# The modulation product of an adaLN block, contracted in chunks of 128, 128, 128 and 64 rows instead of four of 112

## The chip, the cores and the metric

The kernel runs on one core of a Trainium2 chip. The metric is the device time of one execution in microseconds (us). The core has five engines with a queue each, which work their instructions off in order: PE (TensorE, the matrix array; its weight loads are shown apart as PEld), DVE (VectorE), ACT (ScalarE), POOL (GpSimd) and SP (SyncE, which here only issues DMA transfers). ACT's queue issues a few DMAs as well. The queues are shown in the profile as SPq and ACTq where a DMA is issued. SBUF is the on-chip memory with 128 partitions, PSUM the accumulators that PE writes.

## The reference, cut to what matters

```python
def ref(A_x, A_wqkv, A_wo, B_w1, B_b1, B_w2, B_b2, c, w_mod):   # S = 2048, D = 448, F = 1792, H = 16
    mod = (silu(c) @ w_mod).reshape(1, 6, 1, 448)               # c: (1, 448), w_mod: (448, 6 * 448)
    sa, ca, ga, sb, cb, gb = (mod[:, i] for i in range(6))
    h = layernorm(x) * (1 + ca) + sa
    x = x + ga * attention(h, A_wqkv, A_wo)                     # 16 heads of 28, full softmax
    h = layernorm(x) * (1 + cb) + sb
    x = x + gb * (gelu(layernorm(h) @ B_w1 + B_b1) @ B_w2 + B_b2)
    return x
```

All values are float32. The change touches only `silu(c) @ w_mod`: a product of one row of 448 with a matrix of 448 x 2688.

## The kernel before, in words

The order of instructions on every engine is written out by hand in the program; no scheduler reorders it. Tokens are worked in four blocks of 512 (`acc[0]` to `acc[3]`). The first 175 us (phase 1) project q, k and v and take score maxima, the next 580 us or so are attention, the rest is the output projection and the MLP.

**The modulation product before.** The 448 rows of the contraction lie on partitions, in `NC = 4` chunks of `CK = 112`. `c` is loaded as a tile of 112 x 4 (line 132, the first DMA of SP's queue), ACT applies Silu (L138), and DVE copies the result 32 times side by side, so that each chunk is a 112 x 32 weight tile `sil_b` (L293). PE then makes, for each output row of 448 numbers, one matmul per chunk. An output j goes to PSUM partitions 32j to 32j + 31, that is to its own group of 32 columns of the array.

- *First part, `sa` and `ca`* (the shift and scale of the first layernorm): four loads of 112 x 896 at line 154 into `wm_ac`, which lies in the slots c0 and c1 (the profile's `slot_c`). After 24 matmuls that only keep PE busy (L297, they need nothing but the identity), eight matmuls stand at L300, each of them two records in the profile. ACT copies the result out of PSUM (L306), DVE copies 64 of its columns (L307), PE transposes it (L313), and ACT writes the columns `sa_col` and `ca_col` (L316, L317).
- *Second part, `ga, sb, cb, gb`*: `mod_load(k)` at line 562 loads 112 x 1792 into slots v2 and v3, and `mod_mm(k)` makes four matmuls per chunk (L569), one for each of the tasks 0 to 3 of block 1 in phase 1. `mod_fin` brings the result to DRAM and back as rows (L576 to L582).

**The start of the kernel.** SP issues, in this order: `c`, the first half of `acc[0]`, the four loads of `wm_ac`, the q and k weights (L148 to L150), `acc[1]`, the v weights, `acc[2]` and `acc[3]`. ACT's queue issues the second half of `acc[0]`. Eight semaphores go round among the DMAs, so the ninth issue waits until the first transfer has landed, the tenth for the second, and so on. DVE's first work of weight is the copy L293; the layernorm statistics of block 0 (`ln1`, L184 and L185) stand behind it on DVE, then the reciprocal root on POOL (L191), and the normalised tiles come alternately from DVE (L201, L209) and from ACT (L217, L218). On ACT, Silu needs an ACT_TABLE_LOAD ahead of it. ACT's queue then holds: L217, L218, L217, L218, L306, the first weight cast L178, L316, L317, and the copies L282 that apply `sa` and `ca` to the transposed tiles.

On PE the order is L297, L300, eight transposes (L261), L313, eight more transposes, and the q projection (L618, L631, L338). L618 needs the tiles that DVE rounds from L282's output (L285).

The weights of q, k and v are already loaded in the other form: three chunks of 128 rows, and the last 64 rows to both halves of the partitions (L148 to L150).

Of the kernel before, what the change touches and what calls it, by code (L numbers as in the profile page):

```python
# [13 lines left out]
F32 = mybir.dt.float32  # L14
# [8 lines left out]
D = 448  # L23
H = 16
DH = 28
F = 1792
CK = 112
NC = D // CK
NB = S // 512
NG = H // 4  # L30
NKT = S // 128
# [10 lines left out]
def tile_adaln_block(ctx: ExitStack, tc: tile.TileContext, x, wqkv, wo, w1, b1, w2, b2, c, w_mod, out):  # L42
    nc = tc.nc
    pe, act, dve, pool, sp = nc.tensor, nc.scalar, nc.vector, nc.gpsimd, nc.sync
# [27 lines left out]
    def nm(t):  # L72
        uid[0] += 1
        return f"{t}_{uid[0]}"

    def sbt(tag, shape, dt=F32, bufs=1):
        return sb.tile(shape, dt, tag=tag, name=nm(tag), bufs=bufs)

    def slot(tag, shape, dt=F32R):
        return sb.tile(shape, dt, tag="slot_" + tag, name=nm("slot_" + tag), bufs=1)  # L80
# [4 lines left out]
    def slot4(tag, inner):  # L85
        if tag not in halved:
            t = slot(tag, [128, 4] + inner)
            return lambda k: t[:, k]
        t2 = [slot(tag + h, [128, 2] + inner) for h in ("", "h")]
        return lambda k: t2[k // 2][:, k % 2]  # L90
# [6 lines left out]
    def ps_s():  # L97
        return ps_tile("pa", 2)
# [5 lines left out]
    def ps_o():  # L104
        return ps_tile("o")
# [4 lines left out]
    def f(t):  # L110
        return t.bitcast(F32)
# [16 lines left out]


    cols = sbt("cols", [128, 4 * NC])  # L130
    c_col, sil, sa_col, ca_col = cols[:CK, 0:NC], cols[:CK, NC : 2 * NC], cols[:, 2 * NC : 3 * NC], cols[:, 3 * NC :]
    sp.dma_start(c_col, c[0].rearrange("(k p) -> p k", p=CK))
    acc = [sbt(f"acc{b}", [128, 4, D]) for b in range(NB)]

    xv = x[0].rearrange("(b p t) n -> b p t n", p=128, t=4)
    for h in range(2):
        (act if h else sp).dma_start(acc[0][:, 2 * h : 2 * h + 2, :], xv[0][:, 2 * h : 2 * h + 2, :])
    act.activation(sil, c_col, AF.Silu)  # L138

    raw_qk = [slot(f"v{1 + i}", [128, 2, 2 * D], F32) for i in range(2)]  # L140
    raw_v = slot("v3", [128, NC, D], F32)

# [3 lines left out]
    def load_w(cs, dst):  # L146
        for k in range(3):
            sp.dma_start(dst(k), wqkv[128 * k : 128 * k + 128, cs])  # L148
        sp.dma_start(dst(3)[0:64], wqkv[384:D, cs])
        sp.dma_start(dst(3)[64:128], wqkv[384:D, cs])  # L150

    wm_ac = [slot(f"c{i}", [CK, 2, 2 * D], F32) for i in range(2)]
    for k in range(NC):
        sp.dma_start(wm_ac[k // 2][:, k % 2, :], w_mod[k * CK : (k + 1) * CK, 0 : 2 * D])
    load_w(slice(0, 2 * D), lambda k: raw_qk[k // 2][:, k % 2, :])
    sp.dma_start(acc[1], xv[1])
    load_w(slice(2 * D, 3 * D), lambda k: raw_v[:, k, :])
# [5 lines left out]
    wq = [[slot4(f"a{2 * kind + part}", [H, 32]) for part in range(2)] for kind in range(2)]  # L163
    wv = [slot(f"e{part}", [128, NC, D]) for part in range(2)]
    for kind in range(2):
        for part in range(2):
            for k in range(NC):
                pool.memset(f(wq[kind][part](k))[:, :, DH:32], 0.0)
# [120 lines left out]


    d0 = slot("d0", [128, 4, 512], F32)
    sil_b = d0[:CK, 0, 0 : NC * 32].rearrange("p (k r) -> p k r", r=32)
    dve.tensor_copy(sil_b, sil[:, :, None].broadcast_to([CK, NC, 32]))  # L293
    pm = ps_s()
    warm = ps_s()
    for _ in range(WARM):
        pe.matmul(warm[:, :128], ident, ident, start=True, stop=True)  # L297
    for k in range(NC):
        for j in range(2):
            pe.matmul(  # L300
                pm[32 * j : 32 * j + 32, :D], sil_b[:, k, :], wm_ac[k // 2][:, k % 2, j * D : (j + 1) * D],
                start=(k == 0), stop=(k == NC - 1),
            )
    xs0 = ln1(0)
# [253 lines left out]
    mod = {}  # L558

    def mod_load(k):  # L560
        mod[k] = slot(f"v{2 + k % 2}", [128, 4 * D], F32)
        sp.dma_start(mod[k][:CK], w_mod[k * CK : (k + 1) * CK, 2 * D :])

    def mod_mm(k):
        if k == 0:
            mod["p"] = ps_o()
        p = mod["p"]
        for j in range(4):
            pe.matmul(  # L569
                p[32 * j : 32 * j + 32, :D], sil_b[:, k, :], mod[k][:CK, j * D : (j + 1) * D],  # L570
                start=(k == 0), stop=(k == NC - 1),
            )

# [48 lines left out]
    for n, i in (  # L622
# [7 lines left out]
        p, ts = firsts[n]  # L630
# [3 lines left out]
    for b in range(NB):  # L634
# [13 lines left out]
        for n, (tb, kind, g) in enumerate(tasks):  # L648
# [9 lines left out]
            k = n - (6, 5, 4, 4)[b]  # L658
# [16 lines left out]
            if more:  # L675
                k = n - (6, 5, 4, 4)[b]
# [11 lines left out]
            if n == 6:  # L688
                v_init(b)
                if b == 0:  # L690
                    mod_load(0)
                    mod_load(1)
            if b == 2 and n == 5:
                sp.dma_start(b1_col, b1.rearrange("(k p) -> p k", p=128))
            if b == 1:
                if n < 2:
                    mod_mm(n)
                    mod_load(2 + n)
                elif n in (2, 3):
                    mod_mm(n)  # L700
                    if n == 3:
                        mod_fin()
# [348 lines left out]
    def n_maxima(s_):  # L1051
        n_plain, n_wo = left_steps(s_)
        over = len(mxq) - 7 * n_plain // 2
        if is_wo(s_):
            return max(0, -(-over // max(n_wo, 1)))
        plain[0] += 1
        return 4 if plain[0] % 2 or (over > 3 * n_wo and over > 0) else 3
# [11 lines left out]
    for u in range(NU):  # L1069
        g, qt = divmod(u, NB)  # L1070
        for kt in range(NKT):
# [10 lines left out]
            n = n_maxima(step)  # L1082
# [81 lines left out]
    for n in range(len(seq) + LAG):  # L1164
        if n < len(seq):
            b, i = seq[n]
# [38 lines left out]
```

## Time and profile before

| | |
|---|---|
| median of 3 runs | 1142.74 us (1142.39 to 1142.86) |
| profiled execution | 1142.82 us, of which its span 1141.0 us |
| outside the span | 1.8 us |
| PE busy | 1132.1 us, 99% of the span |
| DVE, ACT, POOL busy | 830.5, 680.9, 216.5 us |
| moved by DMA | 81.08 MB, mean 71 GB/s |
| granted PE clock | full in all 40 slices |

The profile shows one execution. Times in it count from the start of the span. In a timeline each line gives start, duration, engine, source line, operation, `out<-in`, the number of instructions merged, and in brackets how long the engine had been idle and what ended that wait. In a view of stretches, each line gives the stretch, the busy time of the engines, the clock, the busy share of the 16 DMA engines and the rate in GB/s. "The chain" is the sequence of work that ended last, traced back from the last instruction.

### The profile page before, as it was taken

How to read it: one execution, taken by the hardware profiler on the slowest of the kernel's cores; microseconds unless marked ns; L12 is line 12 of the kernel's file. 1: busy time of each engine (PE TensorE's matmuls, PEld its weight loads, DVE VectorE, ACT ScalarE, POOL GpSimd, SP SyncE). 2: the span in 40 equal slices, each digit the busy share in tenths (PEclk: the TensorE clock that was granted, in tenths of full speed). 3: DMA queues.
4: the chain of work that ended last, by engine and by line, in shares of the span. 5: the costliest groups of instructions: out<-in, count | busy, mean ns of one | idle time of the engine just before them, and what ended most of it. 6: DMA issues, size and time to landing. Idle time of an engine off the chain costs nothing.

```text
span 1141.0 us, 20798 instructions
## 1 busy us (share of the span) xinstructions
PE 1132.1 (99%) x8380; PEld 682.0 (60%) x8380; DVE 830.5 (73%) x1487; ACT 680.9 (60%) x836; POOL 216.5 (19%) x235
## 2 busy tenths in 40 slices
PE   9999999999999999999999999999999999999998
PEld 7767774444444444444444445545458888888887
DVE  6958788999989899989899977595448853444322
ACT  5666767777877787878787877576862321211110
POOL 2533341110000000000000010207114503123000
PEclk9999999999999999999999999999999999999999
DMA  8652254121231211221111212020423100000000
GB/s 301 205 181 93 94 185 117 51 67 38 67 102 52 62 40 45 78 69 60 52 48 57 91 61 75 11 84 1 135 55 87 43 34 1 1 33 1 33 1 33
DMA packets 49345, 81.08 MB, mean 71 GB/s; under 512 B 12616, under 2 KB 18588, under 8 KB 49248
## 3 DMA queue, kind: packets, MB, share of 16 engines
q1 hardware_dynamic: 48768, 79.01, 22.0%
q8 instruction: 66, 1.08, 0.4%
q10 hardware_dynamic: 144, 0.46, 0.1%
q0 software_dynamic: 336, 0.28, 0.1%
q14 instruction: 31, 0.25, 0.1%
HBM read 53.11 MB, written 26.35 MB: 70 GB/s over the span
## 4 chain that ended last, share of the span: by engine, by line
PE 96%; DVE 1%; DMA 1%; ACT 0%; issue 0%; POOL 0%; DVEq 0%; POOLq 0%; SPq 0%
PE s L1092 27%; PE o L1062 22%; PE m L338 16%; PE pa L338 10%; PE m L415 6%; PE s L1155 4%; PE s L1156 4%; PE s L1154 4%; PE ma L415 1%; PE o L261 1%; PE pa L297 1%; DVE mxp L420 1%; PE m L261 1%; DMA drec<-den 0%; DMA osb<-drec 0%
## 5 line engine op out<-in xcount | busy, mean ns | idle before, releaser
L420 DVE TENSOR_REDUCE mxp<-m 128x1 f32<-128x512 f32 x882 | 556.2, 684 | 105.0 <-PE m L415 79.3
L1092 PE MATMUL s<-slot_b,slot_a 32*128 32x512 f32 x3072 | 384.6, 423 | 0.1
L1097 ACT ACTIVATE slot_c<-s 128x1024 f32<-128x1024 f32 x340 | 329.5, 1022 | 83.7 <-PE s L1092 83.0
L1092 PEld LDWEIGHTS s<-slot_b,slot_a 32*128 32x128 f32 x3072 | 216.2, 183 | 250.9 <-ACT slot_c L1097 148.5
L415 PE MATMUL m<-kh,qh 32*128 32x512 f32 x852 | 282.5, 472 | 0.7 <-DVE mxp L420 0.5
L1097 ACT ACTIVATE slot_d<-s 128x1024 f32<-128x1024 f32 x172 | 166.7, 1021 | 42.0 <-PE s L1092 41.9
L1062 PE MATMUL o<-slot_c,v 128*32 128x512 f32 x1360 | 181.2, 605 | 0.0
L1138 ACT ACTIVATE full<-m,b_col 128x512 f32<-128x512 f32 x56 | 38.5, 688 | 192.1 <-PE m L338 179.8
L1141 DVE CAST hi<-full 128x512 fp32r<-128x512 f32 x56 | 25.2, 450 | 135.4 <-ACT full L1138 135.4
L415 PEld LDWEIGHTS m<-kh,qh 32*128 32x128 f32 x852 | 111.7, 182 | 7.5 <-DVE mxp L420 4.2
L828 POOL TENSOR_TENSOR osb<-osb,osb 128x512 f32<-128x512 f32 x16 | 20.9, 1307 | 445.0 <-DMA osb<-drec 303.0
L1062 PE MATMUL o<-slot_d,v 128*32 128x512 f32 x688 | 92.5, 605 | 0.4 <-ACT osb L1031 0.4
L338 PE MATMUL m<-y,slot_a 128*128 128x512 f32 x160 | 60.6, 395 | 0.0
L1062 PEld LDWEIGHTS o<-slot_c,v 128*32 128x32 f32 x1360 | 26.8, 108 | 54.2 <-issue 52.7
L1142 DVE TENSOR_TENSOR lo<-full,hi 128x512 fp32r<-128x512 f32 x56 | 44.1, 788 | 5.2
L338 PE MATMUL m<-y,slot_c 128*128 128x512 f32 x152 | 47.5, 396 | 0.1
L428 ACT ACTIVATE slot_d<-m 128x512 f32<-128x512 f32 x43 | 24.4, 597 | 37.4 <-PE ma L415 19.7
L1156 PE MATMUL s<-slot_v,lo 128*128 128x448 f32 x128 | 46.7, 365 | 0.0
L1154 PE MATMUL s<-slot_v,hi 128*128 128x448 f32 x128 | 46.6, 364 | 0.0
L338 PE MATMUL m<-y,slot_v 128*128 128x512 f32 x112 | 39.2, 396 | 0.0
L338 PE MATMUL m<-y,slot_b 128*128 128x512 f32 x112 | 39.0, 398 | 0.0
L338 PE MATMUL pa<-slot_c,slot_a 128*128 128x512 f32 x136 | 36.8, 404 | 0.0
(252 smaller groups left out, 1449.6 us busy)
## 6 DMA issues: line engine op xcount, KB each, us to landing
d<-lo SPq DMA_DIRECT2D x32, 256.0 KB
slot_b<-d SPq DMA_DIRECT2D x32, 256.0 KB
slot_a<-d SPq DMA_DIRECT2D x32, 256.0 KB
d<-hi SPq DMA_DIRECT2D x20, 256.0 KB
osb<-drec SPq DMA_DIRECT2D x15, 256.0 KB
out_dram<-xn SPq DMA_DIRECT2D x16, 224.0 KB
slot_v<-in_w_mod_dram SPq DMA_DIRECT2D x4, 784.0 KB
raw<-in_B_w_dram SPq DMA_DIRECT2D x14, 224.0 KB
```

The source lines that it names most:

```text
L338: pe.matmul(p, a, b, start=(i == 0), stop=(i == len(terms) - 1))
L415: pe.matmul(m, qh_sb[(g, qt)][js, i * 128 : (i + 1) * 128], k[js, :], start=True, stop=True)
L420: dve.tensor_reduce(out=mxp[(g, qt)][:, i, j, cch : cch + 1], in_=m, op=ALU.max, axis=AX.X)
L1062: pe.matmul(o[32 * j : 32 * j + 32, :], v_sb[kt // 4][:, kt % 4, 4 * g + j, :], p[:, j, :], start=(kt == 0), stop=(kt == NKT - 1),)
L1092: pe.matmul(s2[:, jj, :], ks[rows_, kp, kc], qs[rows_, qp, :], start=(term == 0), stop=(term == 2))
L1097: act.activation(pt[:, 2 * hf : 2 * hf + 2, :], s2, AF.Exp, scale=SCALE)
L1138: act.activation(gf, p, AF.Gelu_apprx_tanh, bias=b1_col[:, i : i + 1])
L1141: dve.tensor_copy(ghi, gf)
L1142: dve.tensor_tensor(out=glo, in0=gf, in1=f(ghi), op=ALU.subtract)
L1154: pe.matmul(pp, ghi[:, ts], w_hi, start=(m == 0), stop=False)
L1155: pe.matmul(pp, ghi[:, ts], w_lo, start=False, stop=False)
L1156: pe.matmul(pp, glo[:, ts], w_hi, start=False, stop=(m == NFT - 1))
```

## The change

The contraction is cut into chunks of 128, 128, 128 and 64 rows. The last chunk is split by output: the first half of the outputs takes its 64 rows of `w_mod` on partitions 0 to 63, the second half on partitions 64 to 127, and the last 64 numbers of `c` are loaded to both halves. So the last chunk is two loads of 64 rows, each half as wide. The number of matmuls and their widths stay. The loads of `c` move behind the halves of `acc[0]`: 128 x 3 numbers on SP's queue, and two loads of 64 numbers on ACT's queue, ahead of Silu.

```diff
-CK = 112
-NC = D // CK
+NC = 4
...
-    c_col, sil, ... = cols[:CK, 0:NC], cols[:CK, NC : 2 * NC], ...
-    sp.dma_start(c_col, c[0].rearrange("(k p) -> p k", p=CK))
+    c_col, sil, ... = cols[:, 0:NC], cols[:, NC : 2 * NC], ...
...
     for h in range(2):
         (act if h else sp).dma_start(acc[0][:, 2 * h : 2 * h + 2, :], xv[0][:, 2 * h : 2 * h + 2, :])
+
+    sp.dma_start(c_col[:, 0:3], c[0, 0:384].rearrange("(k p) -> p k", p=128))
+    for h in range(2):
+        act.dma_start(c_col[64 * h : 64 * h + 64, 3:4], c[0, 384:D].rearrange("(p k) -> p k", k=1))
     act.activation(sil, c_col, AF.Silu)
...
-    wm_ac = [slot(f"c{i}", [CK, 2, 2 * D], F32) for i in range(2)]
+    def load_mod(dst, k, c0, n):
+        if k < 3:
+            sp.dma_start(dst[:, : n * D], w_mod[128 * k : 128 * k + 128, c0 : c0 + n * D])
+        else:
+            for h in range(2):
+                x0 = c0 + h * n * D // 2
+                sp.dma_start(dst[64 * h : 64 * h + 64, : n * D // 2], w_mod[384:D, x0 : x0 + n * D // 2])
+
+    def mod_part(k, j, n):
+        if k < 3:
+            return slice(0, 128), slice(j * D, (j + 1) * D)
+        h, j = divmod(j, n // 2)
+        return slice(64 * h, 64 * h + 64), slice(j * D, (j + 1) * D)
+
+    wm_ac = [slot(f"c{i}", [128, 2, 2 * D], F32) for i in range(2)]
     for k in range(NC):
-        sp.dma_start(wm_ac[k // 2][:, k % 2, :], w_mod[k * CK : (k + 1) * CK, 0 : 2 * D])
+        load_mod(wm_ac[k // 2][:, k % 2, :], k, 0, 2)
...
-    sil_b = d0[:CK, 0, 0 : NC * 32].rearrange("p (k r) -> p k r", r=32)
-    dve.tensor_copy(sil_b, sil[:, :, None].broadcast_to([CK, NC, 32]))
+    sil_b = d0[:, 0, 0 : NC * 32].rearrange("p (k r) -> p k r", r=32)
+    dve.tensor_copy(sil_b, sil[:, :, None].broadcast_to([128, NC, 32]))
...
         for j in range(2):
+            rs_, cs = mod_part(k, j, 2)
             pe.matmul(
-                pm[32 * j : 32 * j + 32, :D], sil_b[:, k, :], wm_ac[k // 2][:, k % 2, j * D : (j + 1) * D],
+                pm[32 * j : 32 * j + 32, :D], sil_b[rs_, k, :], wm_ac[k // 2][rs_, k % 2, cs],
                 start=(k == 0), stop=(k == NC - 1),
...
-        sp.dma_start(mod[k][:CK], w_mod[k * CK : (k + 1) * CK, 2 * D :])
+        load_mod(mod[k], k, 2 * D, 4)
...
         for j in range(4):
+            rs_, cs = mod_part(k, j, 4)
             pe.matmul(
-                p[32 * j : 32 * j + 32, :D], sil_b[:, k, :], mod[k][:CK, j * D : (j + 1) * D],
+                p[32 * j : 32 * j + 32, :D], sil_b[rs_, k, :], mod[k][rs_, cs],
```

In the changed program the two waits for the small loads of `c` on ACT's queue stand ahead of the ACT_TABLE_LOAD; the wait for the load on SP's queue stands behind it, at Silu itself. On SP's queue the two half loads of the last chunk of `wm_ac` wait for the two halves of `acc[0]`, the q and k weights' first three loads for the three loads of `c`. Elsewhere the order of instructions on every engine is as it was.

More of the change, by code (lines that the diff above doesn't have):

```diff
@@ L130, in tile_adaln_block @@
     cols = sbt("cols", [128, 4 * NC])
-    c_col, sil, sa_col, ca_col = cols[:CK, 0:NC], cols[:CK, NC : 2 * NC], cols[:, 2 * NC : 3 * NC], cols[:, 3 * NC :]
-    sp.dma_start(c_col, c[0].rearrange("(k p) -> p k", p=CK))
+    c_col, sil, sa_col, ca_col = cols[:, 0:NC], cols[:, NC : 2 * NC], cols[:, 2 * NC : 3 * NC], cols[:, 3 * NC :]
     acc = [sbt(f"acc{b}", [128, 4, D]) for b in range(NB)]
```

## The prediction

> **What bounds the kernel now.** I read the page first, then the chain in order of time for the first 31 us, then the timeline of the same stretch, then the DMA rates there, and last the places of the second part. From the page: the span, the busy shares, the clock by slices and the chain by engine.
>
> ```profile
> span 1141.0 us, 20798 instructions
> PE 1132.1 (99%) x8380; PEld 682.0 (60%) x8380; DVE 830.5 (73%) x1487; ACT 680.9 (60%) x836; POOL 216.5 (19%) x235
> PEclk9999999999999999999999999999999999999999
> PE 96%; DVE 1%; DMA 1%; ACT 0%; issue 0%; POOL 0%; DVEq 0%; POOLq 0%; SPq 0%
> ```
>
> PE is the chain almost everywhere, at the full granted clock. So a microsecond added to PE's path at the start, or put between two PE instructions, is a microsecond at the end, and a load that becomes faster behind PE is worth nothing. The change touches two places: the first 16 us, and four short matmul groups between 61 and 75 us. The chain through the first place (start, length, what):
>
> ```profile
> 1.36 8.17 PE pa L297 x48
> 9.53 3.13 PE pa L300 x16
> 12.66 1.02 PE ma L261 x8
> 13.69 0.40 PE pa L313 x4
> 14.11 0.16 ACT cols L316
> 14.38 0.79 ACT raw L282
> 15.19 0.44 DVE slot_b L285
> 15.77 3.40 PE pa L618 x12
> ```
>
> The fillers L297 run to 9.53, then the modulation matmuls, eight transposes, the transposes of the modulation, ACT, DVE, and the first projection. The loads are not in it. The same stretch on the other engines (timeline; in brackets the idle time before and its releaser):
>
> ```profile
> 0.74 0.41 ACTq L137 DMA_DIRECT2D acc<-in_A_x_dram  x1
> 1.19 1.28 ACT L138 ACT_TABLE_LOAD   x1 [1.19 <-PEq L1192]
> 4.57 0.20 ACT L138 ACTIVATE cols<-cols 112x4 f32<-112x4 f32 x1 [2.10 <-DMA cols<-in_c_dram]
> 4.80 0.23 DVE L293 COPY slot_d<-cols 112x128 f32<-112x128 f32 x1 [2.57 <-ACT cols L138]
> 5.57 0.63 DVE L184 BATCH_NORM_STATS2 st<-acc 128x6 f32<-128x448 f32 x1 [0.54 <-DMA acc<-in_A_x_dram]
> 11.08 0.42 ACT L218 ACTIVATE xn<-acc,nm,rs 128x64 f32<-128x64 f32 x1
> 9.87 0.12 PEld L300 LDWEIGHTS pa<-slot_c,slot_d 112*32 112x32 f32 x2 [0.26 <-issue]
> 10.24 0.12 PEld L300 LDWEIGHTS pa<-slot_c,slot_d 112*32 112x32 f32 x2 [0.26 <-issue]
> 11.46 0.11 PEld L300 LDWEIGHTS pa<-slot_c,slot_d 112*32 112x32 f32 x2 [0.35 <-DMA slot_c<-in_w_mod_dram]
> 12.71 0.53 ACT L306 COPY full<-pa 64x448 f32<-64x448 f32 x1 [1.21 <-PE pa L300]
> ```
>
> Two things matter. The layernorm of block 0, which starts at 5.57 with DVE's L184, ends on ACT at 11.50, and ACT then waits 1.21 for PE: this is its slack. And PE itself waited 0.35 once, for the last of the four loads.
>
> **The change, part by part.** *Rates of the loads.* Stretches of the start (rate last):
>
> ```profile
> 4.00:5.50 1.50, 1.00 1.03 404
> 6.00:11.00 5.00, 1.00 1.04 295
> 11.00:14.00 3.00, 1.00 1.03 413
> 14.10:15.60 1.50, 1.00 1.18 280
> ```
>
> By SP's order the first is a 128-row load of x, the second almost wholly the 112-row loads, the third the 128-row weights, the fourth mostly weights of 64 rows. The DMA engines are full in all four. I take 410 GB/s for the three new 128-row loads (1.376 MB, 3.4 us) and 280 for the two half loads (0.229 MB, 0.8 us): 4.2 us, against 1.605 MB at 295, 5.4 us. If the low rate comes from the stride of w_mod and not from the rows, it stays 5.4.
>
> *c behind x.* The small packets of c, in two stretches of 0.5 us:
>
> ```profile
> DMA packets 209, 0.14 MB, mean 274 GB/s; under 512 B 171, under 2 KB 171, under 8 KB 209
> DMA packets 90, 0.17 MB, mean 330 GB/s; under 512 B 44, under 2 KB 44, under 8 KB 90
> ```
>
> They are 3.5 to 4.0 and 2.5 to 3.0: 340 and 88 numbers per us, the slow one beside the large packets of ACT's queue. Both halves of x (0.918 MB) now go first: from about 1.9 at 404 GB/s to 4.2. Then 384 numbers on SP's queue, 1.1 us at the fast rate and 4.4 at the slow one; little runs beside them now, so I take 1.5: to 5.7. The 128 on ACT's queue run beside, to 4.7. Before, the numbers of c were through at about 3.95 and Silu began at 4.57, so 0.6 is added for landing: 5.3 (ACT's) and 6.3 (SP's).
>
> *ACT.* Its two further issues (0.41 each by the first row) end near 2.0, before anything has landed: nothing. But the table load now stands behind the wait for ACT's two loads of c: 5.3 + 1.28 = 6.6, and Silu starts there, as SP's part is in at 6.3. It was 4.57: later by 2.0.
>
> *DVE.* The copy L293 is ahead of the layernorm in the same queue. Silu to copy is 0.23, the copy 0.23: L184 starts at 7.1, not at 5.57, although x is there at 4.8. So the layernorm is later by 1.5. Its steps stay, DVE to POOL to ACT; it ends at 13.0. Bounds: 0.8 if the table load is not held (Silu then follows SP's part of c at 5.9, the fast rate), 4.1 if c takes 4.4 us.
>
> *PE's first part.* The same 16 records. sil_b is ready at 7.1, before the fillers end at 9.53, which covers it; without them PE would wait. The loads land at 5.7 + 4.2 + 0.6 = 10.5 (11.7 at the old rate), so the wait of 0.35 goes and L300 ends near 12.4. What is late next is the layernorm: L306 on ACT starts at 13.0 in place of 12.71, and the transposes L261 wait for the last tile, but end before L307 lets L313 go. Everything from L313 on is later by 1.5 - 1.21 = 0.3 us. The 64-row tiles occur nowhere in this trace; the nearest rows are the 112*32 ones themselves, and I take their time.
>
> *SP's order.* The ninth DMA waits for the first to land: the two half loads issue at about 4.8 and 5.3, the weights from 6.3. Three whole loads stand in the queue until 9, so it does not run dry. The weights land up to 1 us earlier or 0.5 later; the first cast that uses them stands behind L306. Nothing.
>
> *The second part.* One PE group of four, SP's issue around the last load, and the group that uses it:
>
> ```profile
> 61.11 0.96 PE L569 MATMUL o<-slot_v,slot_d 112*32 112x448 f32 x8
> 66.44 0.33 SPq L562 DMA_DIRECT2D slot_v<-in_w_mod_dram  x1
> 67.97 0.32 SPq L384 DMA_DIRECT2D d<-raw  x1
> 73.95 0.96 PE L569 MATMUL o<-slot_v,slot_d 112*32 112x448 f32 x8
> ```
>
> The extra issue (0.33) fits between 66.77 and 67.97, and the load has 7 us where 0.8 MB at 295 GB/s needs 2.7: nothing. If that gap were gone, a write of k to DRAM, read only after 150 us, would be late by 0.33. The four groups keep 0.96.
>
> **Sum.** 0.3 us on the profiled execution: 1142.82 + 0.3 = 1143.1, and as that execution is 0.08 above the median, 1143.0 to 1143.1; I say 1143.1.
>
> **The rivals.** *(B) The halves of the last chunk do not overlap.* In the old rows two outputs (L300) or four (L569) run at once: weight loads at 9.87 and 10.24 are two records in 0.37, each 539 ns. In the changed last chunk the outputs differ in row half as well, and still go to one PSUM bank. If they take turns, L300 ends 0.75 later, at 13.15, costing 0.2 more than the sum (L313 follows eight transposes of 1.02 from there), and the last L569 is longer by 0.75 to 0.96, in full on PE: 1144.1 to 1144.3. For it: in this kernel row groups that run together (L1092) write different banks, so the trace has no such case. Against it: column groups share a bank without loss. The Trainium skill ("TensorEngine Tiling (Array Packing)", Restrictions and Gotchas, Gotcha 1) states this rule: different row tiles cannot access the same PSUM bank at one time. No row here shows it broken or kept.
>
> *(C) The layernorm stays hidden.* If it is late by 1.2 or less (0.8 is the lower bound), L306 starts when L300 ends, and the lost wait of 0.35 is a gain: 1142.4 to 1142.7. It needs a table load that is not held, or c landed by 5.0.
>
> *(D) Slower: c lands late.* The place is the wait of Silu. From a first L184 at 5.57 + 1.21 + 2.29 = 9.07 on, the loss passes 0.2%; that is c landing at 8.6 on SP, or at 7.3 on ACT's queue with the table load behind it. At 88 numbers per us it lands at 4.2 + 4.4 + 0.6 = 9.2, L184 starts at 9.7, the loss is 2.9: 1145.7. The row for it was measured beside large packets of the other queue, which are gone by then; hence unlikely.
>
> *(E) Faster by over 0.2%.* Nothing I find is worth it: the removable wait is 0.35.
>
> **Chances.** Forecast (1142.8 to 1143.9) 0.53; B 0.14; C 0.15; D 0.13; E and unknown gains 0.05. A difference of 0.2% (2.3 us) is about what a measurement of this kernel can tell. Faster 0.05; same 0.53 + 0.14 + 0.15 = 0.82; slower 0.13. The range takes in C with 0.4 for the run and B, and goes to the edge of D: 1142.0 to 1145.0.
>
> **What the changed profile would show.** ACT_TABLE_LOAD at about 5.3, Silu at 6.6, L184 of block 0 at 7.1 (C: before 6.8; D: after 9); no DMA wait in the modulation matmuls; the copy of PSUM on ACT at 13.0, released by the layernorm's work and not by PE; over 400 GB/s while the 128-row loads move; the first projection at 16.1; the last modulation group 0.96 (B: 1.7). Wrong would be a first projection before 15.5 or after 18, or a span that differs by more than the start does.

## The result and the profile after

The changed kernel takes 1144.19 us (median of 22 runs, 1143.84 to 1145.72), the old one 1142.41 (median of 22, 1141.43 to 1143.37): a ratio of 1.0017, interval 1.0010 to 1.0024. That is 1.8 us slower, a real loss; it is under the 0.2% set as the bound, though the interval reaches past it. The forecast was 1143.1 in a range of 1142.0 to 1145.0, with no change beyond 0.2%. Sign and range held; the loss is six times the 0.3 us that the sum gave, so the working has a wrong term.

The page after:

```profile
span 1143.8 us, 20803 instructions
PE 1133.3 (99%) x8380; PEld 684.7 (60%) x8380; DVE 830.5 (73%) x1487; ACT 680.9 (60%) x836; POOL 216.7 (19%) x235
PE 95%; DVE 2%; DMA 2%; issue 1%; ACT 0%; POOL 0%; SPq 0%; DVEq 0%; ACTq 0%; POOLq 0%
```

PE's work grew by 1.2 us of 1132, DVE's and ACT's not at all: the loss is waiting. (The 1.2 us lie at the start, where the granted clock was half for some 3 us: eight transposes took 1.97 instead of 1.09, L637 3.70 instead of 3.40. See the last section.) DMA's share of the chain went from 1 to 2%. The chain in order of time shows where (start, length, what; line numbers are 2 to 19 higher than in the old kernel, L138 is now L140, L184 L201, L300 L318, L618 L637):

```profile
1.19 0.53 ACTq L139
1.75 6.54 DMA cols<-in_c_dram
8.38 0.09 ACT L140
9.68 0.21 ACT cols L140
9.92 0.23 DVE slot_d L310
10.14 0.55 DVE st L201
14.90 0.77 ACT xn L234
15.71 0.77 PE ma L278 x5
16.48 0.55 PE pa L331 x4
18.92 3.49 PE pa L637 x12
```

The fillers and the modulation matmuls are gone from the chain. In their place it begins with the second of the two small loads of c on ACT's queue, which lands at 8.3 us, then the table load, Silu, the copy, and the whole layernorm. The timeline of the same stretch:

```profile
7.01 1.63 SPq L150 DMA_DIRECT2D slot_v<-in_A_wqkv_dram  x3
8.38 1.28 ACT L140 ACT_TABLE_LOAD   x1 [8.38 <-DMA cols<-in_c_dram]
9.68 0.20 ACT L140 ACTIVATE cols<-cols 128x4 f32<-128x4 f32 x1
10.06 0.62 DVE L201 BATCH_NORM_STATS2 st<-acc 128x6 f32<-128x448 f32 x1
10.20 3.32 PE L318 MATMUL pa<-slot_c,slot_d 128*32 128x448 f32 x16 [0.77 <-DVE slot_d L310]
12.57 0.14 PEld L318 LDWEIGHTS pa<-slot_c,slot_d 64*32 64x32 f32 x4 [0.73 <-issue]
15.89 0.51 ACT L324 COPY full<-pa 64x448 f32<-64x448 f32 x1
18.71 3.70 PE L637 MATMUL pa<-slot_b,slot_a 128*128 128x512 f32 x12
76.88 0.96 PE L588 MATMUL o<-slot_v,slot_d 64*32 64x448 f32 x8
```

The first projection L637 starts at 18.71 where L618 started at 15.77: 2.94 us late. The last modulation group started at 73.95 and now at 76.88: the second part adds nothing. The profiled execution (1145.62 us) lies 1.4 above its kernel's median. How its lateness develops can be read off ACT's copies that end the 16 attention units, old then new (last column pair: first and last start; then the fifteenth copy alone):

```profile
L1031 ACT COPY osb<-o x16: 585/587/595, 219.8 to 846.2; 128x512 f32<-128x512 f32 x16
801.90 0.59 ACT L1031 COPY osb<-o 128x512 f32<-128x512 f32 x1
```

```profile
L1050 ACT COPY osb<-o x16: 586/587/592, 222.5 to 849.2; 128x512 f32<-128x512 f32 x16
803.57 0.59 ACT L1050 COPY osb<-o 128x512 f32<-128x512 f32 x1
```

It is 2.6 late at the first copy, 1.7 at the fifteenth, 2.9 at the last. In the same comparison the other kernels run below, whatever they change, gain 0.3 to 1.0 us on this execution of the old kernel between the first and the fifteenth copy; from there to the last some gain another 0.1 to 0.2 and others fall back by 0.5 to 1.4. So these steps seem to go with the execution and not with the change; what the change moved is the start. What makes the steps stays open.

### The profile page after: what moved, and what is told of

The parts are those of the page before. It is cut to its first block, busy times and chain, and to the rows that moved or that the text cites. A ratio compares the mean times of both kernels' runs of the same rounds, so it can differ in the third digit from the quotient of the medians.

```text
span 1143.8 us, 20803 instructions
## 1 busy us (share of the span) xinstructions
PE 1133.3 (99%) x8380; PEld 684.7 (60%) x8380; DVE 830.5 (73%) x1487; ACT 680.9 (60%) x836; POOL 216.7 (19%) x235
## 4 chain that ended last, share of the span: by engine, by line
PE 95%; DVE 2%; DMA 2%; issue 1%; ACT 0%; POOL 0%; SPq 0%; DVEq 0%; ACTq 0%; POOLq 0%
PE s L1111 27%; PE o L1081 22%; PE m L356 16%; PE pa L356 10%; PE m L433 6%; PE s L1174 4%; PE s L1175 4%; PE s L1173 4%; PE ma L433 1%; PE o L278 1%; DMA osb<-drec 1%; DVE mxp L438 1%; DMA cols<-in_c_dram 1%; DMA drec<-den 1%; PE m L278 1%
## 5 line engine op out<-in xcount | busy, mean ns | idle before, releaser
L356 PE MATMUL m<-y,slot_a 128*128 128x512 f32 x160 | 60.6, 395 | 0.0
L356 PE MATMUL m<-y,slot_c 128*128 128x512 f32 x152 | 47.5, 396 | 0.1
L356 PE MATMUL m<-y,slot_v 128*128 128x512 f32 x112 | 39.2, 396 | 0.0
L356 PE MATMUL m<-y,slot_b 128*128 128x512 f32 x112 | 39.0, 398 | 0.0
L356 PE MATMUL pa<-slot_c,slot_a 128*128 128x512 f32 x136 | 36.8, 404 | 0.0
```

The source lines that it names most:

```text
L356: pe.matmul(p, a, b, start=(i == 0), stop=(i == len(terms) - 1))
```

## The experiments

Two theories stood. *Late c*: the loss is the late Silu, because c is loaded behind x, because its 128 four-byte numbers on ACT's queue take turns with large packets, because the table load stands behind their wait, and because the layernorm stands behind Silu's result on DVE. *Chunk form*: the 64-row tiles, the extra loads, or the later weights cost the time. Ratios are to the old kernel on the same chip.

**c first, new chunks.**

```diff
+    sp.dma_start(c_col[:, 0:3], ...)          # before the halves of acc[0]
+    for h in range(2): act.dma_start(c_col[64 * h : 64 * h + 64, 3:4], ...)
     for h in range(2):
         (act if h else sp).dma_start(acc[0][:, 2 * h : 2 * h + 2, :], ...)
```

> The three loads of c are put ahead of the halves of x again, on the same two queues; the chunks of 128, 128, 128 and 64 rows stay. Theory 'late c' (the loss is the late Silu, whose loads of c trickle beside large packets; layernorm start minus 6.8 us is lost): Silu starts by 6, the first statistics by 6.5, the first projection between 15.3 and 16.0, and the time is that of the old kernel within 0.5 us (1.0000 plus or minus 0.0005). Rival 'chunk form' (the 64-row tiles, the two more loads and the weights that are issued later cost the time): Silu is early and the kernel still 1.8 us slower than the old one (1.0016).

Measured 0.9995 (0.9986 to 1.0004), 1141.56 us.

```profile
5.61 1.28 ACT L140 ACT_TABLE_LOAD   x1 [5.61 <-DMA cols<-in_c_dram]
6.90 0.20 ACT L140 ACTIVATE cols<-cols 128x4 f32<-128x4 f32 x1
16.10 3.41 PE L637 MATMUL pa<-slot_b,slot_a 128*128 128x512 f32 x12 [0.67 <-DVE slot_b L302]
```

Silu is later than expected (6.9), the projection 0.1 later, but the loss is gone with the 64-row tiles, the extra loads and the second part all in place. The chunk form costs nothing that can be measured.

**Table load early.**

```diff
+    act.activation(sil[:, 0:1], zero_col, AF.Silu)
     act.activation(sil, c_col, AF.Silu)
```

> As the changed kernel, but a Silu of one column of zeros stands ahead of the real one on ACT, so that the ACT_TABLE_LOAD runs at the start and not behind the loads of c. Late c: Silu follows the landing of c at once, about 1.3 us earlier than in the changed kernel for the same landing; the loss falls from 1.8 to about 0.5 us (1.0005). Chunk form: no change, 1.0016.

```profile
2.39 1.28 ACT L140 ACT_TABLE_LOAD   x1 [2.39 <-issue]
8.41 0.20 ACT L141 ACTIVATE cols<-cols 128x4 f32<-128x4 f32 x1 [4.53 <-DMA cols<-in_c_dram]
17.39 3.40 PE L638 MATMUL pa<-slot_b,slot_a 128*128 128x512 f32 x12 [0.68 <-DVE slot_b L303]
```

c lands at the same time, Silu comes 1.27 earlier and the projection 1.32 earlier, as expected. The measured ratio fell less, to 1.0012 (1.0003 to 1.0021); the expected 1.0005 lies within that interval.

**All of c on SP's queue, behind x.**

```diff
-        act.dma_start(c_col[64 * h : 64 * h + 64, 3:4], ...)
+        sp.dma_start(c_col[64 * h : 64 * h + 64, 3:4], ...)
```

> As the changed kernel, but the two small loads of c are issued on SP's queue, behind the large load of c, and not on ACT's queue. Late c, where the 128 numbers on ACT's queue are what trickles beside the modulation weights on SP's queue: they land with the rest of c, near 7, Silu starts at 8.3 and not at 9.7, and about 1 us of the loss goes in the profile. If c is late only because it is behind x, Silu stays near 9.7 and the time at 1.0016.

1.0013 (1.0004 to 1.0022).

```profile
7.46 1.28 ACT L140 ACT_TABLE_LOAD   x1 [7.46 <-DMA cols<-in_c_dram]
8.75 0.21 ACT L140 ACTIVATE cols<-cols 128x4 f32<-128x4 f32 x1
17.73 3.39 PE L637 MATMUL pa<-slot_b,slot_a 128*128 128x512 f32 x12 [0.68 <-DVE slot_b L302]
```

The projection starts 0.98 earlier than in the changed kernel, as expected; in the time only 0.3 to 0.5 of it shows. So standing on the other queue, beside the modulation weights, costs 0.9 at the start. Most of the rest goes when c is put ahead of x.

**Each number twice on ACT's queue.** The dose test for the turns.

```diff
-        act.dma_start(c_col[64 * h : 64 * h + 64, 3:4], c[0, 384:D]...)
+        act.dma_start(cols[64 * h : 64 * h + 64, 3:5]..., c[0, 384:D]...[:, None, :].broadcast_to([64, 2, 1]))
```

> As the changed kernel, but each of the two small loads of c on ACT's queue brings every number twice (64 x 2 four-byte numbers in place of 64 x 1; the second copy is overwritten by Silu's output). If these numbers are late because each takes its turn with a large packet of the modulation weights on the other queue, twice as many land about 2 us later (10 to 10.5 in place of 8.3) and the loss grows by about 2 us: 1.0030 to 1.0036. If the lateness is a latency of small loads, whatever their count, nothing changes: 1.0016.

1.0032 (1.0020 to 1.0044).

```profile
9.83 1.28 ACT L140 ACT_TABLE_LOAD   x1 [9.83 <-DMA cols<-in_c_dram]
11.12 0.20 ACT L140 ACTIVATE cols<-cols 128x4 f32<-128x4 f32 x1
20.09 3.39 PE L637 MATMUL pa<-slot_b,slot_a 128*128 128x512 f32 x12 [0.67 <-DVE slot_b L302]
```

The last landing moves by 1.45 (2 were expected), and Silu and projection by 1.44 and 1.38. Which load is late can be read from the semaphores in the trace: each load adds to its semaphore as its sixteen parts land, and the last of them counts. In the changed kernel the large load was in at 6.83, ACT's first small load at 6.99 and its second at 8.29; with each number twice at 6.75, 6.91 and 9.74. So the first small load, which moves beside the numbers of the large one, lands no later with twice the count. The second, which moves beside the modulation weights, comes 1.30 behind the first with 64 numbers and 2.83 with 128: about 45 to 50 numbers per us. That part of the lateness goes with the count and is no fixed latency. The Trainium skill ("DMA: Bandwidth & Descriptors", Queues, rings and completion order) says that a DMA engine goes round the queues that it has work for and drains a whole packet, typically some 9 to 17 descriptors, before it switches. By that, if the numbers spread evenly over sixteen engines, the four or eight of one engine could pass in a single turn (an estimate from that page); here twice the numbers took 2.2 times as long, and the measurement decides. The turns themselves no view shows.

**Only c moved, old chunks.**

```diff
-    sp.dma_start(c_col, c[0].rearrange("(k p) -> p k", p=CK))     # ahead of x
+    sp.dma_start(c_col, c[0].rearrange("(k p) -> p k", p=CK))     # behind the first half of x
```

> The old kernel (four chunks of 112, one load of c on SP's queue), with the load of c behind the first half of x and nothing else changed. Late c: c lands near 7, Silu follows it without a table load, the statistics start near 7.5, and 0.7 us is lost (1.0006). Chunk form: the time is that of the old kernel, 1.0000 plus or minus 0.0003.

1.0013 (1.0004 to 1.0022): most of the loss without any new chunk. The expected Silu is there, but something else ends last:

```profile
6.77 0.21 ACT L138 ACTIVATE cols<-cols 112x4 f32<-112x4 f32 x1 [4.31 <-DMA cols<-in_c_dram]
11.58 0.95 PE L300 MATMUL pa<-slot_c,slot_d 112*32 112x448 f32 x4 [0.60 <-DMA slot_c<-in_w_mod_dram]
13.07 0.95 PE L300 MATMUL pa<-slot_c,slot_d 112*32 112x448 f32 x4 [0.54 <-DMA slot_c<-in_w_mod_dram]
14.06 0.53 ACT L306 COPY full<-pa 64x448 f32<-64x448 f32 x1 [0.98 <-PE pa L300]
17.12 3.39 PE L618 MATMUL pa<-slot_b,slot_a 128*128 128x512 f32 x12 [0.67 <-DVE slot_b L285]
```

c delays the 112-row loads behind it, PE waits twice for them, and the projection is 1.35 late, not 0.7. In the changed kernel this wait is absent: its 128-row loads move faster, and PE comes to them only at 10.20. With c first and the new rows Silu came at nearly the same time as here (6.90) and the projection 1.02 earlier (16.10): the new rows seem to hide part of what the new place of c costs, though the place of c differs between these two runs as well.

**Layernorm ahead of the copy on DVE.**

```diff
+    xs0 = ln1(0)
     dve.tensor_copy(sil_b, sil[:, :, None].broadcast_to([128, NC, 32]))
...
-    xs0 = ln1(0)
```

> As the changed kernel, but the layernorm of block 0 is issued on DVE ahead of the copy of Silu's result, not behind it. Late c through DVE's queue: DVE and POOL work on the layernorm from 5; ACT's part still stands behind Silu (8.4 to 9.9 in the changed kernel's profile), so the normalised tiles are done near 12.2 and not at 16.0, the modulation matmuls end near 13.7, and the copy of PSUM is near 13.8 in place of 15.9: about 2 of the 2.9 us of the start are gained back, and the time is within 0.5 us of the old kernel (1.0000 plus or minus 0.0005). If the matmuls alone were late for c, the order on DVE would change nothing: 1.0016.

1.0006 (0.9997 to 1.0015). That is just outside the expected band of 0.0005, whose edge lies within the interval: about 1.2 us of the loss goes by the order on DVE alone. The profiled execution (1144.2, its median is 1142.97) shows a further thing. Timeline, and then stretches (length, PE's busy time, its granted clock, share and rate of DMA):

```profile
5.30 0.63 DVE L201 BATCH_NORM_STATS2 st<-acc 128x6 f32<-128x448 f32 x1 [3.06 <-DMA acc<-in_A_x_dram]
10.82 4.97 PE L319 MATMUL pa<-slot_c,slot_d 128*32 128x448 f32 x16 [2.00 <-DVE slot_d L311]
```

```profile
9.00:10.80 1.80, 0.00 (x0) 1.00 1.10 296
12.00:15.50 3.50, 3.50 (x12) 0.51 1.06 343
```

PE waited 2.0 us for the copy, and 1.2 us after that wait had ended the clock was half for 3.5 us: the 16 records took 4.97 instead of 3.32, and the start gained nothing in this execution (the projection came at 18.89). That the gain of the median comes from executions with the full clock is likely and not shown.

**Small loads of c first, the large one behind x.**

```diff
+    for h in range(2): act.dma_start(c_col[64 * h : 64 * h + 64, 3:4], ...)   # ahead of x
     (act if h else sp).dma_start(acc[0][:, 2 * h : 2 * h + 2, :], ...)
     sp.dma_start(c_col[:, 0:3], ...)
```

> As the changed kernel, but the two small loads of c on ACT's queue stand ahead of the second half of x; the large load of c on SP's queue stays behind the first half. If the small loads are late because they take turns with the modulation weights' large packets, they now land before 5, the table load is through by then or soon after, and Silu starts when the large load of c lands, near 7: the first projection near 16.6 (0.8 later than the old kernel), the time 0.3 to 0.8 us above it (1.0003 to 1.0007). If only the place behind x counts for all of c alike, Silu stays near 8 or later and the time at 1.0012 to 1.0016.

1.0007 (0.9999 to 1.0016).

```profile
7.23 1.28 ACT L140 ACT_TABLE_LOAD   x1 [7.23 <-DMA cols<-in_c_dram]
17.50 3.40 PE L637 MATMUL pa<-slot_b,slot_a 128*128 128x512 f32 x12 [0.67 <-DVE slot_b L302]
```

The time came, the way did not. The large load and the first small one were in by 4.6; what the table load waited for is the second small load, issued at 1.32, which landed at 7.17, although it stands ahead of x on its queue. Fifteen of its sixteen parts were in by 5.6; why the last took until 7.2 stays open. Silu starts at 8.53 and the projection at 17.50, 0.9 later than expected, so this run does not show where the small loads have to stand.

**c as rows, turned by PE; 24 and 16 fillers.** `c` comes as four rows of 128 numbers, PE transposes them among the fillers, Silu reads PSUM.

```diff
+    sp.dma_start(c_row[0:3], c[0, 0:384].rearrange("(k p) -> k p", p=128))
+    act.dma_start(c_row[3:4]..., c[0:1, None, 384:D].broadcast_to([1, 2, 64]))
...
+            pe.transpose(c_ps[:, 0:4], c_row, ident[:4, :4])     # after 8 fillers
+    act.activation(sil, c_ps[:, 0:4], AF.Silu)
```

> New chunks, but c comes as four rows of 128 numbers (two transfers of a few large packets, ahead of x, the last row the 64 numbers twice), and PE transposes them into a column tile after 8 of the 24 fillers; Silu reads that from PSUM. Late c, and c's 512 four-byte packets as its price: c lands by 3.5, Silu starts by 4.5 with no table load in its way, x lands near 5, the statistics start near 5.2, the modulation weights land by 9.5, the matmuls start with the end of the fillers and end near 12.5; the first projection starts near 15.5, 0.2 to 0.3 earlier than in the old kernel, and the time is 0.2 to 1.0 us below it (0.9991 to 0.9998). Chunk form as the cause: no faster than the old kernel.

> The same with 16 fillers in place of 24. If the start is then bound by the landing of the modulation weights and by the layernorm (end near 11.0), the matmuls start near 6.7 and end near 10.5, the copy of PSUM starts near 11, the first projection near 14.1: 1.7 us earlier than the old kernel, time 1140.6 to 1141.0 (0.9984 to 0.9988). If the fillers are needed to bring PE to speed, the modulation matmuls and transposes take longer than 0.37 us a pair and up to 1 us of that is lost.

0.9997 (0.9989 to 1.0006), in the expected band, and 1.0002 (0.9993 to 1.0010), a miss. Silu starts at 5.38 and 5.13, 0.9 and 0.6 later than expected, and the second half of x, on ACT's queue behind a load of c, keeps the statistics waiting until 7.83 and 8.09. The projection starts at 16.05 and 14.94. The second is 0.83 ahead of the old kernel, and the 11 times (1141.5 to 1144.0) show nothing of it. In the profiled execution it is still there at the end (a span of 1140.0 for 1141.0); why the others don't show it stays open.

**Two more combinations.** First, c first with the table load early (both diffs above). Second, c as rows with `sp.dma_start(c_row[3:4]...)` in place of `act.dma_start`, and `WARM = 20`.

> New chunks, the three loads of c ahead of the halves of x (as in the run with c first), and the ACT_TABLE_LOAD drawn to the start by a Silu of one column of zeros. With c first Silu started at 6.9, 1.3 of it the table load behind the landing at 5.6. Late c: Silu at 5.6, statistics from 6.1, layernorm done at 12.0; the modulation matmuls (end near 13, set by the landing of their weights) are then what is late, so the first projection comes only 0.1 to 0.3 earlier than with c first, at 15.8 to 16.0, and the time is 0.5 to 1.0 us below the old kernel (0.9991 to 0.9996).

> c as rows of 128 numbers, both transfers on SP's queue, x's second half alone on ACT's queue, 20 fillers. If the late second half of x (its statistics waited until 7.8 in the runs with c as rows) came from standing behind a load of c on ACT's queue and then taking turns with the modulation weights, it lands by 6 here, the layernorm ends near 11.3, the modulation matmuls near 11.5, the copy of PSUM starts near 11.6, and the first projection near 14.6: 1.1 us ahead of the old kernel, time 0.9985 to 0.9995.

0.9999 (0.9990 to 1.0008) and 1.0001 (0.9992 to 1.0010). Both miss: the projections start at 16.13 and 16.33. In the first Silu comes at 5.75, but the second half of x, behind the small loads on ACT's queue, holds the statistics until 8.92. In the second the modulation weights land late (PE waits 0.37 and 0.72). What is gained on one load is lost on another, and no version is measurably faster than the old kernel; the lowest is the one with c first.

The six kernels with the new chunks whose start hangs on Silu, in one table: when the three loads of c had landed, and how much later than in the old kernel the first projection started (profile) and the kernel ended (median, same chip):

| | large load | small loads | projection | time |
|---|---|---|---|---|
| c first | 2.88 | 3.04, 5.52 | +0.33 | -0.76 |
| table load early | 6.83 | 6.99, 8.31 | +1.62 | +1.42 |
| small loads first | 4.63 | 4.18, 7.17 | +1.73 | +0.53 |
| all of c on SP's queue | 6.00 | 6.30, 7.37 | +1.96 | +1.53 |
| changed | 6.83 | 6.99, 8.29 | +2.94 | +1.78 |
| each number twice | 6.75 | 6.91, 9.74 | +4.32 | +3.46 |

In all six the second small load is the last. The time follows the start, with 0.2 to 1.2 us less; that difference no run explains.

## Why the prediction was right and where it was wrong

In the six kernels with the new chunks in which the layernorm stands behind Silu and sets the start (changed, c first, table early, c on SP, small loads first, numbers twice), the projection starts 9.0 to 9.2 us after Silu: 18.71 - 9.68, 16.10 - 6.90, 17.39 - 8.41, 17.73 - 8.75, 17.50 - 8.53, 20.09 - 11.12. So Silu's start is the term on which all hangs.

- *c behind x: the step that failed.* The sum let ACT's two loads land at 5.3 and SP's at 6.3. SP's was in at 6.83; ACT's at 6.99 and 8.29, and the second set the start, 3.0 late. The sentence "little runs beside them now" was wrong: rival D was priced by a row measured beside large packets and called unlikely as these "are gone by then", but the modulation weights follow on SP's queue at once. The mechanism was named and its row quoted; the mistake was to ask only what is in front of c, and not what follows it on the other queue. That is not all of the 3.0: with all of c on one queue 0.9 is given back. x was in at 5.4 where the sum has 4.8. For the remaining 1.5 the likely cause is that the sum let ACT's numbers pass beside SP's without delay; with all 512 on one queue the last were not in before 7.37. No run shows this part alone.
- *ACT's table load behind the wait:* right. 1.28 us, and taking it away gave 1.3 back in the profile. But the order of the waits, as told under the change and used in the sum, is not that of the trace: ahead of the table load stand the waits for the large load and for the second small one, and the wait for the first small one stands at Silu. By the sum's own landings the table load would then begin at 6.3, Silu at 7.6, and the loss would be 1.3 and not 0.3. In the changed kernel this made no difference, as the second small load came last.
- *DVE's order, layernorm behind the copy:* right. The statistics started 0.4 after Silu (0.5 was worked out), but at 10.1 and not at 7.1: 4.5 late, of which the slack of 1.21 leaves 3.3; 2.94 was lost at the projection, where 0.3 was said. Rival D said 2.9 for c at 9.2 on SP's queue; it came by ACT's queue and the table load instead.
- *The time:* D's place and mechanism came true with D's loss at the start, but the median moved by 1.8, under the 2.3 from which D was to decide. By the prediction's own mark the loss passes 0.2% when L184 starts after 9.07, and it started at 10.06; the first projection, at 18.71, lies beyond the 18 named there as a sign of being wrong. The profiled execution did lose 2.8. The prediction's premise was that a microsecond at the start is a microsecond at the end; that the median lost one less than the start is in no term of the sum: the forecast of no change beyond 0.2% held by luck.
- *Rates of the loads:* right. Two stretches of the changed kernel in which 128-row modulation weights move, with little beside them in the second:

```profile
6.00:7.00 1.00, 1.00 (x9) 1.00 (x8) 0.00 (x0) 0.00 (x0) 0.00 (x0) 1.00 0.75 233
7.00:9.00 2.00, 2.00 (x20) 2.00 (x20) 0.00 (x0) 0.61 (x1) 0.00 (x0) 1.00 1.01 400
```

  400 GB/s against 295 for 112 rows of the same matrix: it is the rows, not the stride. Until 7 the numbers of c still hold the rate down.
- *Rival B, two row halves in one PSUM bank:* refuted. The last group of L588 has 64*32 tiles and takes 0.96, as with 112 rows; L318 takes 3.32 for 3.20. The rule of the Trainium skill ("TensorEngine Tiling (Array Packing)", Gotcha 1) that was weighed there was to cost 0.75 in the first place and 0.75 to 0.96 in the second, and no run shows such a cost. What does come with the 64-row tiles in L318 is a start at 12.57 where the rhythm of 0.37 gave 12.10; why stays open.
- *Rival C, the layernorm hidden:* not in the changed kernel. With c first it nearly is.
- *SP's order and the second part at nothing:* right; L588 keeps its distance from the start.

## What to carry to other kernels

A load of a few hundred four-byte numbers is not small to a DMA queue: ask what stands ahead of it, what runs on the other queue while it moves, and which of several such loads comes last. Where an engine's first work waits for such a load, all that is queued behind it waits as well, here a layernorm that needed nothing from it. When several changes lie in one, measure the moved load and the new form apart: here the form was free, and its place in the order cost it all.

## What the runs showed of the hardware that was not expected

- Loads on 112 partitions moved at 295 GB/s, on 128 at 400 to 413, and a stretch of mostly 64-partition loads at 280, with the DMA engines' share at 1.0 or above in all.
- 128 four-byte numbers behind x on ACT's queue needed until 8.3 us; doubling them added 1.45 us, all of it on the second load, which moved beside the modulation weights.
- After waits of PE the granted clock fell to half for some 3 us, in the profiled executions of two kernels: after a wait of 2.0 us in the one with the layernorm ahead, and in the changed kernel after a stretch of 3 us with PE busy for 1.58 (length, PE's busy time, its granted clock, share and rate of DMA):

```profile
13.00:16.00 3.00, 1.58 (x10) 1.00 1.05 300
17.00:20.00 3.00, 3.00 (x12) 0.50 1.01 404
```

  The Trainium skill ("TensorE: Matmul & The Clock Gate", Part 1) puts the bound at an idle window of about 3.4 us; the wait of 2.0 us was shorter, and the measurement decides. A wait of 2.06 us in the profiled execution of the kernel with doubled numbers did not bring it on. In the changed kernel it cost nothing in the end: the projection started as late after Silu as in the kernels whose clock stayed full. L637 took 3.70 where theirs took 3.40, but L356 behind it starts at 27.56, 8.85 after L637, and with c first at 24.95, 8.85 after it too.
